# A column sum moved from TensorE to GpSimd, and four PSUM evictions split between ScalarE and GpSimd

## The chip, the cores and the metric

The kernel runs on one core of one Trainium2 chip. The metric is the time of one execution on the device in microseconds (us); the number that stands for a kernel is the median of several runs. A core has five engines with a queue of instructions each, which run in the order in which they were written: TensorE (PE in the profile, with its weight loads as PEld), VectorE (DVE), ScalarE (ACT), GpSimd (POOL) and SyncE (SP, which here only issues DMAs). POOL issues DMAs too. An instruction waits on semaphores for what it needs, and everything behind it on its engine waits with it.

## What is computed

The reference first does a small attention between x (8 batches, 8 heads, 512 positions, 64 wide) and a state of 32 slots, in both directions; its outputs, put together, are 8 x 544 = 4352 rows of 512. On these rows it runs a two-layer network:

```python
h = x @ w_in                 # 512 -> 2048
r = np.maximum(h, 0.0)
g = s * (r * r) + b          # s and b: one number each
return (g @ w_out)           # 2048 -> 512
```

Since b is one number, `g @ w_out` is `s * (r*r) @ w_out + b * colsum(w_out)`, where `colsum` adds the 2048 rows of w_out. The second term is one row of 512 numbers, the same for every output row. The kernel computes it once as `bias_bc`, repeated on all 128 partitions, and adds it where the products leave PSUM.

## The kernel before

The work goes batch by batch (b = 0 to 7). For each batch the attention weights are computed from `xT` (x transposed) and `stT` (`att_scores`, `att_M`), and layer 1 multiplies the weights `a4` with `M` (state times w_in, `L267 ... bank<-a,M` in the profile), which gives h without the attention's output ever being formed. ACT evicts h with a relu (L921), DVE squares it in place (L931): this is `g`, held in f16. Layer 2 multiplies g with w_out, which lies in four tiles `wo[0]` to `wo[3]`, each [128 partitions, 4 blocks, 512 columns] in f16, loaded by four DMAs from POOL's queue (L433).

Batch 0's layer 2 (`layer2_first`, L1134) is a plain product: 16 blocks of w_out times four row blocks `rr`, into two banks of the kind `o` and two of the kind `ps`. The other batches use `layer2` (L1187), a scheme with seven instead of eight block products, which needs sums of blocks of w_out (`weight_sums`, L1040, tile `u`, made by DVE once, line L1051) and of blocks of g (`pair_sums`, L1004, tile `pd`, by DVE, lines L1013, L1021, L1024). What leaves PSUM there is multiplied by s and joined with the bias by DVE (`take`, L1222) or with an earlier part (`give`, L1234), into one of six f32 tiles `osb`, and sent to memory by a DMA (`put`, L1128). The attention's second direction (`att_turn`, `att_reads`) transposes the weights by DMA into `aT` (L835, on SP) and multiplies them with x into a bank `V`; its results are collected in `srd` by a copy on POOL (L880) and pass through the network at the end. Before the transposes of batches 0 and 1 POOL writes two columns of `aT` from `wo[3]` (L828), so that the transposes start after that load.

`bias_sum` (L1086) makes the bias in six operations. PE sums w_out's rows with a weight of ones of 32 columns, sixteen matmuls, four at a time beside each other in the array, so that every column sum stands on 32 partitions four times over in parts (L1101). ACT copies it to f16 (L1102), DVE makes the remainder (L1105), so that two f16 numbers hold the f32 sum. PE adds over the partitions with weights of 1/32 (`thirty2`, L1116), and DVE multiplies with b (L1119).

No order is written by hand. All of this only hands operations to a planner (`Plan`, L27). An operation names the engines that may run it with a cost in us, the keys that it reads and writes, and a priority; a lower number goes first. `order` (L84) walks through time: of the operations that could start earliest it takes the one with the best priority, within a small room, and books its cost:

```python
rank = (t + shy, o.prio, o.n)
if best is None or rank < best[0]:
    best = rank, o, e, t
...
room = t + (self.ROOM if e == "PE" else 0.02)
```

DMAs after 35 us are given 4.4 us to land (`LATE`), and buffers are freed by these planned times. The instructions then stand in each engine's queue in the order of the plan; on the chip they keep it, whatever their true times. A cost in the plan thus moves an instruction's place in the queues, not its time. The priorities around the change: the relus of batch 1 2.51, its squares and products of layer 1 4.01, the sums of `weight_sums` 5.5, `pair_sums` 6, the products of `layer2_first` 9, `put` 20, the L828 copies 30.

Of the kernel before, what the change touches and what calls it, by code (L numbers as in the profile page):

```python
# [26 lines left out]
class Plan:  # L27
# [36 lines left out]
    def op(self, engs, fn, rd=(), wr=(), prio=5, mode=None, dma=0.0, gap=0.0, into=(), lands=None):  # L64

        o = Op(len(self.ops), engs, fn, rd, [*wr, *((u,) for u in into)], prio, mode, dma, gap)
        o.lands = lands
        for key in rd:
            o.before.update(self.wrote[key])
        for key in wr:  # L70
            o.before.update(self.wrote[key])
            o.before.update(self.read[key])
        for key in rd:
            self.read[key].append(o)
        for key in wr:
            self.wrote[key] = [o]
            self.read[key] = []
        o.before.discard(o)
        for u in o.units:
            self.users[u].append(o)  # L80
        self.ops.append(o)
        return o
# [146 lines left out]
def kernel(  # L229
# [10 lines left out]
    nc = tc.nc  # L240
    AF = mybir.ActivationFunctionType
    ALU = mybir.AluOpType

    B, H, S, D = x.shape
    Ns = state.shape[2]
    DM = H * D
    DF = moe_w_in.shape[1]
    P = 128
    NKM = DM // P
    NKF = DF // P  # L250
# [5 lines left out]
    scale = float(1.0 / np.sqrt(D))  # L256
# [6 lines left out]
    def sb(name, shape, dtype=FP16):  # L263
        return pool.tile([P, *shape], dtype, name=name, tag=name)

    def mm(out, lhsT, rhs, start=True, stop=True, tp=None, is_transpose=None):
        return nc.tensor.matmul(  # L267
            out,
            lhsT,
            rhs,  # L270
            start=start,
            stop=stop,
            tile_position=tp,
            is_transpose=is_transpose,
            skip_group_check=True,
        )

    ps = [psum.tile([P, FC], FP32, name=f"bank_{i}", tag=f"bank_{i}") for i in range(6)]
# [18 lines left out]
    plan = Plan()  # L297
# [16 lines left out]
    wo = [sb(f"wo_{q}", [4, DM]) for q in range(4)]  # L314
# [6 lines left out]
    gate = sb("gate", [2])  # L321
    ident16 = sb("ident16", [P])
    bones16 = sb("bones16", [P])
    ones16 = sb("ones16", [Ns])
    thirty2 = sb("thirty2", [P])
    one = sb("one", [1], FP32)
    sb1 = sb("sb1", [2], FP32)
    sb_row = sb("sb_row", [2, P], FP32)
# [1 line left out]
    s_bc, b_bc = sb_bc[:, 0:1], sb_bc[:, 1:2]  # L330
    bias_bc = sb("bias_bc", [DM], FP32)
    wsp = sb("wsp", [2, DM])

    ident_dr = nc.inline_tensor(np.eye(P, dtype=np.float16), name="ident_const")
    bones_dr = nc.inline_tensor(
# [5 lines left out]
    nc.vector.memset(warm, 0.0)  # L341
    nc.vector.memset(ones16, 1.0)
    nc.vector.memset(one, 1.0)
    nc.vector.memset(thirty2, 1.0 / Ns)

    def warm_up():
        mm(ob[1], warm[:, 0:P], warm)
# [7 lines left out]
    def T(u):  # L355
        return plan.tile(u)

    op = plan.op
    K = lambda u, *sub: (u, *sub)
# [105 lines left out]
    for i in range(4):  # L465
# [4 lines left out]
        wr=[K(("bones",))],  # L470
        prio=0,
        lands=8.2,
    )
    for i, src in enumerate((moe_s, moe_b)):
        op(
            {"SP": 0.5},
            lambda e, i=i, src=src: nc.sync.dma_start(sb1[0:1, i : i + 1], src.unsqueeze(0)),
            wr=[K(("sb1", i))],
            prio=0,
# [408 lines left out]
    def g_view(u):  # L888
        return T(u).rearrange("p (f t) -> p f t", f=4)
# [194 lines left out]
        )  # L1084

    def bias_sum():  # L1086
        u = plan.unit(("wsum",), "ps")

        def t(e):
            for i in range(NKF // 4):  # L1090
                for q in range(4):
                    mm(
                        T(u)[32 * q : 32 * q + 32],
                        ones16,
                        wo[i][:, q, :],
                        start=(i == 0),
                        stop=(i == NKF // 4 - 1),
                        tp=(0, 32 * q),
                    )

        op({"PE": 0.87}, t, rd=[K(("wo", q)) for q in range(4)], wr=[K(u)], prio=2, mode="cols")  # L1101
        op({"ACT": 0.52}, lambda e: nc.scalar.copy(wsp[:, 0], T(u)), rd=[K(u)], wr=[K(("hi",))], prio=1)  # L1102
        op(
            {"DVE": 0.66},
            lambda e: nc.vector.tensor_tensor(wsp[:, 1], T(u), wsp[:, 0], ALU.subtract),  # L1105
            rd=[K(u), K(("hi",))],
            wr=[K(("lo",))],
            prio=1,
        )
        v = plan.unit(("bias",), "ps")  # L1110

        def t2(e):
            for i in range(2):
                mm(T(v), thirty2, wsp[:, i], start=(i == 0), stop=(i == 1))

        op({"PE": 0.43}, t2, rd=[K(("hi",)), K(("lo",))], wr=[K(v)], prio=2, mode="full")  # L1116
        op(
            {"DVE": 0.66},
            lambda e: nc.vector.tensor_scalar(bias_bc, T(v), b_bc, None, ALU.mult),  # L1119
            rd=[K(v), K(("b",))],  # L1120
            wr=[K(("bias_bc",))],
            prio=1,
        )

    def put(dst, src, key, prio, last=False):
        op(
            {"SP": 0.6} if last else {"POOL": 0.6},
            lambda e: eng(e).dma_start(dst, src()),  # L1128
            rd=[key],
            prio=prio,  # L1130
            dma=0.75,
        )

    def layer2_first():  # L1134

        us = [plan.unit(("o", 0, i), "o" if i < 2 else "ps") for i in range(4)]

        for q in range(4):
            for f in range(4):
                for rr in range(4):  # L1140

                    def t(e, q=q, rr=rr, f=f):
                        mm(
                            T(us[rr]),
                            g_view(G[0, q])[:, f, P * rr : P * rr + P],
                            wo[q][:, f, :],
                            start=(q == 0 and f == 0),
                            stop=(q == 3 and f == 3),
                        )

                    op(
                        {"PE": 0.2157},
                        t,
                        rd=[K(("wo", q)), K(G[0, q], f // 2)],
                        wr=[K(us[rr])],
                        prio=9 + 0.2 * rr if q == 3 else 9,
                        mode="full",
                    )
        for rr in range(4):
            t = plan.unit(("osb", 0, rr), "osb")  # L1160
            op(
                {"DVE": 0.66},
                lambda e, t=t, rr=rr: nc.vector.scalar_tensor_tensor(  # L1163
                    T(t), T(us[rr]), s_bc, bias_bc, ALU.mult, ALU.add
                ),
                rd=[K(us[rr]), K(("s",)), K(("bias_bc",))],
                wr=[K(t)],
                prio=0,
            )
            put(  # L1170
                out_BSn[0, 0:S].rearrange("(q c) n -> c q n", c=SCH)[2 * (rr % 2) + rr // 2],
                lambda t=t: T(t),
                K(t),
                20,
            )
# [140 lines left out]
    layer1(0)  # L1316
    numbers()
    bias_sum()
    layer2_first()
    layer1(1)  # L1320
    for q in range(4):
# [67 lines left out]
```

## Time and profile before

| | us |
|---|---|
| median of 3 runs (210.03 to 210.66) | 210.12 |
| profiled execution, its own time | 209.61 |
| its span, first to last instruction | 207.8 |
| L267 bank<-wo,ones, 16 matmuls, first start | 31.25 |
| L1102 on ACT | 0.59 |
| L1105 on DVE | 0.68 |
| L1119 on DVE | 0.75 |
| L1163 on DVE, four times, 44.77 to 48.24 | 0.75 each |
| L828 on POOL, four copies, first start | 30.60 |
| L1222, first of `layer2(1)` | 49.11 |

The span is what the trace covers; the 1.8 us beside it are before the first and after the last instruction. Busy times are unions of an engine's instructions. Lines of the timeline give the start, the length, the engine, the line, the operation, what is written and read, and the number of instructions that are merged; consecutive instructions of one engine overlap, so the step from one start to the next is shorter than the length of one. All matmuls have the line L267, a helper's, and are told apart by their tiles. The clock that TensorE was granted is 0.998 of full speed.

### The profile page before, as it was taken

Reading aid. Unit: us, or ns where it says so; the run is one execution under the profiler, and the core shown is the slowest. Engines: PE = TensorE matmul, PEld = TensorE weight load, DVE = VectorE, ACT = ScalarE, POOL = GpSimd, SP = SyncE. Lnnn points to the kernel's source line nnn. Section 1 sums busy time; section 2 is a strip of 40 time slices with the busy share of each in tenths; the row PEclk is TensorE's granted clock in tenths of the full one; section 3 lists DMA queues with packets and bytes.
Section 4 is the critical chain, followed back from the end, with each engine's and each line's share of the span. In section 5 each row is a group of like instructions: output and inputs, shape, how many; then the busy total and the mean of one; then the engine's idle time right before and its main releaser. Section 6 shows DMA issues by size and latency. Waiting matters only on the chain.

```text
span 207.8 us, 4869 instructions
## 1 busy us (share of the span) xinstructions
PE 200.2 (96%) x1968; PEld 132.2 (64%) x1968; DVE 167.3 (80%) x330; ACT 116.7 (56%) x264; POOL 39.4 (19%) x66
## 2 busy tenths in 40 slices
PE   7988999999999999999999999999999999999991
PEld 2434334448864674578477747774777478888881
DVE  1476679999996999999989799988898799684461
ACT  4595699900278689764964596369635953130000
POOL 5930010015113110212301205620105011210000
PEclk9999999999999999999999999999999999999999
DMA  6999999526847843298581841696105101112132
GB/s 187 228 200 206 206 192 150 96 42 175 179 107 155 128 110 78 57 152 195 112 105 58 148 109 52 77 260 79 51 9 162 44 6 50 54 50 101 54 126 76
DMA packets 41930, 24.04 MB, mean 116 GB/s; under 512 B 26292, under 2 KB 40116, under 8 KB 41908
## 3 DMA queue, kind: packets, MB, share of 16 engines
q0 software_dynamic: 15296, 15.40, 38.9%
q1 hardware_dynamic: 25940, 8.17, 19.5%
q8 instruction: 15, 0.25, 0.5%
q10 hardware_dynamic: 672, 0.16, 0.4%
q14 instruction: 7, 0.06, 0.1%
HBM read 17.37 MB, written 8.91 MB: 126 GB/s over the span
## 4 chain that ended last, share of the span: by engine, by line
PE 84%; DMA 8%; DVE 4%; POOL 2%; issue 0%
PE o L267 45%; PE bank L267 39%; DMA wi<-in_moe_w_in_dram 7%; DVE osb L1163 1%; DMA ident<-ident_const 1%; DVE osb L1222 1%; POOL wi L420 1%; DVE pd L1013 1%; POOL xn L407 0%; POOL wo L433 0%; DVE osb L1234 0%; DVE pd L1024 0%; DVE pd L1021 0%; DVE u L1051 0%; POOL gate L457 0%
## 5 line engine op out<-in xcount | busy, mean ns | idle before, releaser
L921 ACT ACTIVATE g<-bank 128x512 f16<-128x512 f32 x128 | 64.3, 653 | 11.6 <-PE bank L267 11.4
L267 PE MATMUL bank<-a,M 128*128 128x512 f16 x256 | 58.2, 379 | 0.3 <-DVE a L785 0.3
L267 PEld LDWEIGHTS <-pd 128*128 128x128 f16 x480 | 46.2, 98 | 10.5 <-issue 3.1
L931 DVE TENSOR_TENSOR g<-g 128x1024 f16<-128x1024 f16 x64 | 43.7, 689 | 8.4 <-ACT g L921 8.4
L267 PEld LDWEIGHTS <-g 128*128 128x128 f16 x424 | 41.0, 98 | 13.6 <-issue 1.3
L267 PE MATMUL o<-u,pd 128*128 128x256 f16 x360 | 43.3, 273 | 0.3 <-DVE osb L1222 0.2
L267 PEld LDWEIGHTS <-M 128*128 128x128 f16 x256 | 24.7, 98 | 29.5 <-issue 1.6
L1128 POOL DMA_DIRECT2D out_dram<-osb x28 | 18.5, 659 | 109.2 <-DVE osb L1234 68.9
L267 PE MATMUL o<-wo,g 128*128 128x256 f16 (+1 forms) x272 | 38.0, 285 | 0.0
L1222 DVE SCALAR_TENSOR_TENSOR osb<-o,sb_bc,bias_bc 128x512 f32<-128x512 f32 (+1 forms) x32 | 22.8, 717 | 8.1 <-PE o L267 7.6
L365 DVE CAST M<-bank 128x512 f16<-128x512 f32 x36 | 23.6, 684 | 4.9 <-PE bank L267 4.9
L726 ACT ACTIVATE E<-bank 128x256 f16<-128x256 f32 x28 | 10.4, 384 | 29.6 <-PE bank L267 29.6
L1234 DVE SCALAR_TENSOR_TENSOR osb<-o,sb_bc,osb 128x512 f32<-128x512 f32 (+1 forms) x24 | 17.2, 715 | 5.7 <-PE o L267 5.6
L365 ACT CAST M<-bank 128x512 f16<-128x512 f32 x28 | 15.3, 596 | 10.2 <-PE bank L267 10.2
L1013 DVE TENSOR_TENSOR pd<-g 128x1024 f16<-128x1024 f16 (+1 forms) x32 | 20.6, 652 | 0.2
L267 PE MATMUL o<-u,g 128*128 128x256 f16 x120 | 15.5, 273 | 0.0
L267 PE MATMUL o<-wo,pd 128*128 128x256 f16 x120 | 15.3, 273 | 0.0
L1024 DVE TENSOR_TENSOR pd<-g,pd 128x512 f16<-128x512 f16 (+1 forms) x32 | 13.0, 409 | 0.1
L1021 DVE TENSOR_TENSOR pd<-g,pd 128x512 f16<-128x512 f16 (+1 forms) x32 | 12.8, 404 | 0.1
L267 PE MATMUL bank<-wi,stT 64*32 64x512 f16 x256 | 10.8, 382 | 1.1 <-DMA wi<-in_moe_w_in_dram 1.1
L976 ACT ACTIVATE g<-bank 128x512 f16<-128x512 f32 x8 | 4.8, 597 | 11.0 <-PE bank L267 11.0
L267 PE MATMUL bank<-wo,g 128*128 128x512 f16 x32 | 9.7, 380 | 0.0
(63 smaller groups left out, 137.4 us busy)
## 6 DMA issues: line engine op xcount, KB each, us to landing
out_dram<-osb POOLq DMA_DIRECT2D x28, 256.0 KB, 3.1
xn<-in_x_dram POOLq DMA_DIRECT2D x7, 512.0 KB, 6.8
wi<-in_moe_w_in_dram POOLq DMA_DIRECT2D x4, 512.0 KB, 11.1
wo<-in_moe_w_out_dram POOLq DMA_DIRECT2D x4, 512.0 KB, 17.8
u<-in_x_dram SPq DMA_DIRECT2D x4, 256.0 KB, 3.8
out_dram<-osb SPq DMA_DIRECT2D x4, 256.0 KB, 2.5
out_dram<-osb SPq DMA_DIRECT2D x4, 128.0 KB, 2.3
xT<-xn SPq DMA_TRANSPOSE x24, 3.2
```

Of the source, the lines that this page charges most:

```text
L267: return nc.tensor.matmul(out, lhsT, rhs, start=start, stop=stop, tile_position=tp, is_transpose=is_transpose, skip_group_check=True,)
L365: (nc.scalar.copy if e == "ACT" else nc.vector.tensor_copy)(dst, src)
L726: lambda e, g=g, m=m: nc.scalar.activation(T(E[b])[:, g, hS * m : hS * m + hS], T(("T", b, m))[:, hS * g : hS * g + hS], AF.Exp, scale=sca ...
L921: lambda e, u=u, j=j, i=i: nc.scalar.activation(g_view(G[b, j])[:, i], T(u), AF.Relu),
L931: nc.vector.tensor_mul(t, t, t)
L976: lambda e, u=u, two=two: nc.scalar.activation(two(), T(u), AF.Relu),
L1013: nc.vector.tensor_tensor(view()[:, :, 0:2], blocks(b, j)[:, :, 1:2, :].to_broadcast((P, 2, 2, n)), blocks(b, j)[:, :, 0:4:3, :], ALU.subt ...
L1021: nc.vector.tensor_tensor(view()[:, :, 2], blocks(b, j)[:, :, 3], view()[:, :, 0], ALU.subtract)
L1024: nc.vector.tensor_tensor(view()[:, :, 3], blocks(b, j)[:, :, 2], view()[:, :, 2], ALU.subtract)
L1128: lambda e: eng(e).dma_start(dst, src()),
L1222: lambda e: nc.vector.scalar_tensor_tensor(t_view(u), o_view(bank), s_bc, bias(h), ALU.mult, ALU.add),
L1234: lambda e: nc.vector.scalar_tensor_tensor(t_view(u), o_view(bank), s_bc, t_view(u), ALU.mult, ALU.add),
```

## The change

`bias_sum` no longer sums on PE. Fifteen additions on POOL run through the sixteen blocks of w_out into an f32 tile `wacc`, which is the memory of `bias_bc`; each reads and writes all of `wacc`. They have the priority 12 and a planned cost of 1.1. Every partition then holds the sum of its own 16 rows, so the two matmuls over the partitions take plain ones as weights and `thirty2` goes. The operations behind have priority 4 where they had 1 or 2.

In `layer2_first` the four products leave PSUM by ACT, multiplied by s alone, into `osb`, and POOL adds `bias_bc` in place (priority 19, planned cost 1.3) before the DMA. `layer2` is not touched.

```diff
-    ones16 = sb("ones16", [Ns])
-    thirty2 = sb("thirty2", [P])
+    ones16 = sb("ones16", [P])
...
+    wacc = bias_bc
...
-    nc.vector.memset(thirty2, 1.0 / Ns)
...
-        op({"PE": 0.87}, t, rd=[K(("wo", q)) for q in range(4)], wr=[K(u)], prio=2, mode="cols")
-        op({"ACT": 0.52}, lambda e: nc.scalar.copy(wsp[:, 0], T(u)), rd=[K(u)], wr=[K(("hi",))], prio=1)
+        blocks_ = [(q, f) for q in range(4) for f in range(4)]
+        for i, (q, f) in enumerate(blocks_):
+            if i == 0:
+                continue
+            one_ = (lambda: wo[0][:, 0]) if i == 1 else (lambda: wacc)
+            op(
+                {"POOL": 1.1},
+                lambda e, q=q, f=f, one_=one_: nc.gpsimd.tensor_tensor(wacc, one_(), wo[q][:, f], ALU.add),
+                rd=[K(("wo", q))],
+                wr=[K(("wacc",))],
+                prio=12,
+            )
+        op({"ACT": 0.52}, lambda e: nc.scalar.copy(wsp[:, 0], wacc), rd=[K(("wacc",))], wr=[K(("hi",))], prio=4)
...
-            lambda e: nc.vector.tensor_tensor(wsp[:, 1], T(u), wsp[:, 0], ALU.subtract),
+            lambda e: nc.vector.tensor_tensor(wsp[:, 1], wacc, wsp[:, 0], ALU.subtract),
...
-                mm(T(v), thirty2, wsp[:, i], start=(i == 0), stop=(i == 1))
+                mm(T(v), ones16, wsp[:, i], start=(i == 0), stop=(i == 1))
...
-                {"DVE": 0.66},
-                lambda e, t=t, rr=rr: nc.vector.scalar_tensor_tensor(
-                    T(t), T(us[rr]), s_bc, bias_bc, ALU.mult, ALU.add
-                ),
-                rd=[K(us[rr]), K(("s",)), K(("bias_bc",))],
+                {"ACT": 0.6},
+                lambda e, t=t, rr=rr: nc.scalar.activation(T(t), T(us[rr]), AF.Copy, scale=s_bc),
+                rd=[K(us[rr]), K(("s",))],
                 wr=[K(t)],
                 prio=0,
+            )
+            op(
+                {"POOL": 1.3},
+                lambda e, t=t: nc.gpsimd.tensor_tensor(T(t), T(t), bias_bc, ALU.add),
+                rd=[K(("bias_bc",))],
+                wr=[K(t)],
+                prio=19,
             )
```

More of the change, by code (lines that the diff above doesn't have):

```diff
@@ L1086, in bias_sum @@
     def bias_sum():
[L1087 to L1099, printed above, removed]
-        op({"PE": 0.87}, t, rd=[K(("wo", q)) for q in range(4)], wr=[K(u)], prio=2, mode="cols")
-        op({"ACT": 0.52}, lambda e: nc.scalar.copy(wsp[:, 0], T(u)), rd=[K(u)], wr=[K(("hi",))], prio=1)
+        blocks_ = [(q, f) for q in range(4) for f in range(4)]
[11 more added lines that the diff above has]
+        op({"ACT": 0.52}, lambda e: nc.scalar.copy(wsp[:, 0], wacc), rd=[K(("wacc",))], wr=[K(("hi",))], prio=4)
         op(
             {"DVE": 0.66},
-            lambda e: nc.vector.tensor_tensor(wsp[:, 1], T(u), wsp[:, 0], ALU.subtract),
-            rd=[K(u), K(("hi",))],
+            lambda e: nc.vector.tensor_tensor(wsp[:, 1], wacc, wsp[:, 0], ALU.subtract),
+            rd=[K(("wacc",)), K(("hi",))],
             wr=[K(("lo",))],
-            prio=1,
+            prio=4,
         )
@@ L1113, in t2 @@
             for i in range(2):
-                mm(T(v), thirty2, wsp[:, i], start=(i == 0), stop=(i == 1))
-        op({"PE": 0.43}, t2, rd=[K(("hi",)), K(("lo",))], wr=[K(v)], prio=2, mode="full")
+                mm(T(v), ones16, wsp[:, i], start=(i == 0), stop=(i == 1))
+        op({"PE": 0.43}, t2, rd=[K(("hi",)), K(("lo",))], wr=[K(v)], prio=4, mode="full")
         op(
@@ L1120, in bias_sum @@
             rd=[K(v), K(("b",))],
-            wr=[K(("bias_bc",))],
-            prio=1,
+            wr=[K(("bias_bc",)), K(("wacc",))],
+            prio=4,
         )
```

## The prediction

> **What bounds the kernel now.** I read the page's busy shares first, then the chain of waits between 40 and 54 us, then the timelines of TensorE (PE), VectorE (DVE) and GpSimd (POOL) in the stretch that the change touches.
>
> The busy shares and the first shares of the chain:
>
> ```profile
> PE 200.2 (96%) x1968; PEld 132.2 (64%) x1968; DVE 167.3 (80%) x330; ACT 116.7 (56%) x264; POOL 39.4 (19%) x66
> ...
> PE 84%; DMA 8%; DVE 4%; POOL 2%; issue 0%
> ```
>
> PE is the bound. The windows show it busy 182.94 of the 183.32 us from 20.38 to 203.70, so a PE instruction that goes is worth its full step, and a wait put into PE's queue costs its full length. The 4% of DVE lie in one place. In the chain's answer for 40 to 54 us (start, length, what):
>
> ```profile
> 44.77 0.75 DVE osb L1163
> 45.52 0.33 DVE u L1051
> 45.86 1.40 DVE osb L1163 x2
> 47.25 0.33 DVE pd L1021
> 47.58 0.66 DVE osb L1163
> ...
> 51.13 0.67 DVE osb L1234
> 51.80 0.04 issue
> 51.84 2.13 PE o L267 x18
> ```
>
> DVE runs without a pause from 44.77, and PE waits at 51.84 for its L1234 (0.15 us). DVE work done before 51.84 therefore has no slack here, although PE itself is hardly idle.
>
> **The PE part.** The timeline of PE around the removed sum:
>
> ```profile
> 29.64 1.67 PE L267 MATMUL bank<-a,M 128*128 128x512 f16 x7
> 31.25 1.05 PE L267 MATMUL bank<-wo,ones 128*32 128x512 f16 x16
> 32.23 1.04 PE L267 MATMUL bank<-a,M 128*128 128x512 f16 x4
> ```
>
> The seven matmuls step by 0.22 us, so the last starts at 30.94 and the next could start at 31.16 instead of 32.23: **1.07 us** less, mode changes included. The later two bias matmuls (34.61, 0.59 us with `thirty2`) stay, with `ones16` as weights. The matmuls behind need `a` (L794, 29.89 to 30.57) and are ready. The memset of `thirty2` (165 ns at the start) goes beside loads and counts nothing.
>
> **The GpSimd additions: their length.** Fifteen additions of 128x512 replace the sixteen matmuls. POOL has no addition in this trace. The low end is DVE's step for a f32 tile of that size, 0.67 us (45.86 to 47.25 holds two). The high end is POOL's own copies: five of 128 columns start between 127.8 and 130.1, 0.58 us apart; four of 2 columns between 30.6 and 31.1, 0.17 apart; the slope, 3.3 ns a column, makes 1.85 us of 512. These copies write with gaps and read one input, an addition writes densely and reads two. I take the middle, 1.3. [...]
>
> When they run: the `wo` loads take 11.5 to 21.0 us to landing. The last lands at 30.5 (issue 9.54 plus 21.0, and POOL's L828 starts at 30.60); the one before, issued at 8.38, at about 28 (the median of 17.8 and its place between put it there). Additions on earlier quarters run from about 17 us and are done by then. The last eight can start at 28: 28 + 8 x 1.3 = 38.4 undisturbed.
>
> **What they do to DVE** decides the case. The one place where POOL computes over more than 2 columns beside DVE shows this (POOL first, then DVE):
>
> ```profile
> 127.77 3.30 POOL L880 COPY srd<-srdT 128x128 f16<-128x128 f16 x5
> ```
> ```profile
> 127.42 0.51 DVE L1021 TENSOR_TENSOR pd<-g,pd 128x512 f16<-128x512 f16 x1
> 127.86 0.88 DVE L931 TENSOR_TENSOR g<-g 128x1024 f16<-128x1024 f16 x1
> ...
> 128.91 0.75 DVE L1222 SCALAR_TENSOR_TENSOR osb<-o,sb_bc,bias_bc 128x512 f32<-128x512 f32 x1
> 129.58 0.68 DVE L365 CAST M<-bank 128x512 f16<-128x512 f32 x1
> 130.17 0.55 DVE L1024 TENSOR_TENSOR pd<-g,pd 128x512 f16<-128x512 f16 x1
> ```
>
> L1021 and L1024 otherwise take 0.42, L931 0.68. The operations with two SBUF inputs are stretched by 0.09, 0.20 and 0.13; those that read PSUM keep their 0.75 and 0.68. A fourth at 170.78 (0.51 instead of 0.42) meets the copy at 171.1. That is about 0.1 us for each copy of 128 columns and one input. An addition reads eight times as many columns, so some 0.75 us of DVE if it lies wholly beside such operations. The ends are 0.1 (a fixed price per instruction) and the whole 1.3; nothing in an added POOL read makes DVE faster, so a gain is excluded. I take 0.75, which scales the row. [...]
>
> From 28 to 41 us DVE is busy 11.9 us (4.17, 4.77 and 5.00 in the windows of 5 us from 28, 33 and 38); less the casts (1.29), `wsp` (0.68) and bias (0.75), about 9.2 of 13 us are two-SBUF operations (L931, L1051, L794), a share of 0.71. Eight additions: 8 x 0.75 x 0.71 = 4.3 us. DVE's idle time there is about 1 us, mostly ahead of 31; I count half as usable: **DVE is 3.8 us late** at 41 us. POOL is held too, by about as much: 28 + 8 x (1.3 + 0.5) = 42.4.
>
> **How this reaches PE.** The queues are written in the order of the planner, which knows no contention and counts 1.1 us per addition. ACT's copy to `wsp` has a lower claim than the relus; ACT's run of relus ends at 41.17, now 40.1. So in the plan: copy 40.1 (0.59), DVE's subtraction (0.68), with two handovers of 0.2, and the bias matmuls at 41.8. Behind them in PE's queue stand the rest of the first batch's layer 2 and all that follows. In truth the subtraction stands behind DVE's late work, 3.8 us late (POOL's chain alone would make it some 2.3 late), and PE waits about **3.8 us** at the bias matmuls. Copy and subtraction now read SBUF instead of PSUM; the nearest rows from SBUF, ACT's 0.71 (L804) and DVE's 0.75 for a f32 tile, differ by 0.1, which I leave out. ACT has nothing else until the four evictions, so its wait costs only them.
>
> **The evictions.** Four DVE operations (0.75, step 0.70) go, 2.8 us, with the idle 0.41 before the first about 3.0 of DVE's queue ahead of 51.84. ACT is idle from 41.17 to 55.75, so four of about 0.6 (`wsp`'s copy: 0.59) are free. Four POOL additions come in 45 to 52, beside DVE's `pd` sums: 4 x 0.75 x 0.7 = 2.1 back. PE would come 1.07 earlier, so of the 3.0 there are 1.9 for it: 0.2 us more late.
>
> **What is moved.** POOL's four L828 copies (30.60) stand behind the additions by their priority, so the four aT transposes on SP come some 12 us later and the V matmuls (40.53) with them; the planner knows that to 37, adds 4.4 us to a landing, and V's result is used at the end: nothing. Output DMAs start after the additions, 2 to 4 us later, x_load of batch 3 (48.10) likewise; its transposes run only at 66: nothing. Six `osb` buffers are held longer, which may hold back one `take` at 55 by 1 to 2 us; other matmuls fill that.
>
> **Sum**: -1.07 + 3.8 + 0.2 = about +3.0 us. The profiled execution (span 207.8, its own time 209.61) would be 212.6; on the runs' median of 210.12 this is **213.1**.
>
> **Rivals.** *The other side: faster.* If a POOL read costs DVE only a fixed 0.1 to 0.2 an instruction, the loss is 8 x 0.15 x 0.71 = 0.9, less 0.5 usable: 0.4 of wait at the bias matmuls, the chain (38.4 and a bit) comes before 40.1, and the relieved DVE removes the 0.15 wait: -1.07 + 0.4 - 0.15 = -0.8, **209.3**; with no wait at all 208.9. It decides from a loss under 0.2 to 0.25 us an addition, and additions under 1.6 us (28 + 8 x 1.6 = 40.8). For it speaks that only about 0.1 was ever seen; against it that it grew with overlap (0.20 beside two copies). Chance 0.27.
> *Exclusion*: each addition takes its 1.3 from DVE: 8 x 1.3 x 0.71 - 0.5 = 6.9, then 4 x 1.3 x 0.7 - 1.9 = 1.7: -1.07 + 8.6 = +7.5, **217.6**. Chance 0.15.
> *It cancels*: the wait eats the 1.07 (loss of 0.3 an addition): 210.1. Chance 0.08.
> *My forecast*, a loss of 0.4 to 0.9 or additions of 1.7 us or more: 211 to 216, chance 0.50.
>
> **The numbers.** The runs tell 0.3% (0.6 us) from no change: faster 0.27, within 0.08, slower 0.65. The range takes in the fast rival and most of exclusion, 208.8 to 217.6; the likeliest case's own is 211 to 216.
>
> **What would show it.** No wo,ones matmuls and a step of 0.22 in their place; POOL additions back to back from 17 us, steps of 1.3 to 1.9 after 28; L931 and L1051 stretched over 0.8 and 0.5 beside them; L1105 after 44 and a PE idle time of 3 to 4 us whose releaser is DVE `wsp`; no PE wait at `pd` beyond 0.5. Wrong if L931 stays at 0.68 to 0.75 beside additions: then PE has no new wait and it is faster. An addition of 2 us or more would make POOL, through ACT's L1102 copy, the releaser.

## The result and the profile after

The changed kernel takes 218.26 us (median of 4 runs, 217.71 to 219.16), the kernel before 210.07 in the same comparison: a ratio of 1.039, 95% interval 1.0367 to 1.0414. The forecast was slower, 213.1, in a range of 208.8 to 217.6. The direction holds, the time lies above the range.

From the page of the changed kernel: the busy times, PE's row and the granted clock in 40 slices, and the chain by engine.

```profile
PE 201.8 (93%) x1952; PEld 132.2 (61%) x1952; DVE 175.1 (81%) x325; ACT 119.6 (55%) x268; POOL 70.1 (32%) x85
PE   7889999909799999999999999999999999999992
PEclk9999999975999999999999999999999999999999
PE 74%; DVE 12%; DMA 7%; POOL 2%; ACT 1%; issue 1%; DVEq 0%
```

PE has 16 instructions less and is busy 1.6 us longer. Its row has one empty slice (43 to 48 us), and the clock falls beside and behind it. DVE's share of the chain has gone from 4 to 12%.

PE's timeline shows where (start, length, what, and in brackets the idle time and what ended it):

```profile
43.09 0.38 PE L267 MATMUL bank<-wsp,ones 128*128 128x512 f16 x1
48.51 0.59 PE L267 MATMUL bank<-wsp,ones 128*128 128x512 f16 x1 [5.04 <-DVE wsp L1102]
48.89 1.49 PE L267 MATMUL o<-wo,g 128*128 128x512 f16 x3
50.17 3.28 PE L267 MATMUL bank<-wo,g 128*128 128x512 f16 x8
...
57.24 0.82 PE L267 MATMUL o<-u,pd 128*128 128x256 f16 x6
59.47 0.84 PE L267 MATMUL bank<-ident,st 128*128 128x128 f16 x12 [1.41 <-DVE st L514]
```

The same places in the kernel before:

```profile
34.61 0.59 PE L267 MATMUL bank<-wsp,thirty 128*128 128x512 f16 x2
45.44 1.89 PE L267 MATMUL bank<-wo,g 128*128 128x512 f16 x8
```

The first bias matmul runs, the second waits 5.04 us for DVE's subtraction (L1102, L1105 before). The eight matmuls into `bank` at 50.17 take 3.28 us; before, the same eight took 1.89. Their step is 0.43 instead of 0.22. The windows give the granted clock of this stretch as 0.50 (half speed):

```profile
core 0: us, PE busy (x) PEld busy (x) DVE busy (x) ACT busy (x) POOL busy (x), PEclk, DMA share, GB/s
46.20:52.90 6.70, 4.39 (x11) 1.61 (x11) 6.70 (x16) 1.38 (x2) 2.36 (x1) 0.50 0.00 0
```

The sum, by starts: 5.42 us from the first bias matmul to the second instead of 0.22, 5.2 lost; 4.56 us for the eleven steps from 48.51 to 53.07 instead of 2.4, 2.2 lost to the clock; 1.57 at 59.47 (six steps of 0.11 behind 57.24 end at 57.90). Against that the removed matmuls: the last matmul of batch 0's layer 1 and the first of batch 1's stand 0.38 us apart (31.05 and 31.43) instead of 1.29 (30.94 and 32.23), 0.91 gained. Together +8.1; the spans differ by 8.1 (215.9 and 207.8).

Why DVE is late stands in POOL's and in its own timeline:

```profile
22.84 16.57 POOL L1094 TENSOR_TENSOR bias_bc<-bias_bc,wo 128x512 f32<-128x512 f32 x12 [1.40 <-DMA wo<-in_moe_w_out_dram]
```
```profile
30.00 1.37 DVE L793 TENSOR_TENSOR a<-E,a 128x1024 f16<-128x1024 f16 x1
31.29 1.37 DVE L1050 TENSOR_TENSOR u<-wo 128x512 f16<-128x512 f16 x1
32.59 1.64 DVE L930 TENSOR_TENSOR g<-g 128x1024 f16<-128x1024 f16 x1
34.15 1.38 DVE L1050 TENSOR_TENSOR u<-wo,u 128x512 f16<-128x512 f16 x1
...
38.31 1.37 DVE L1050 TENSOR_TENSOR u<-wo,u 128x512 f16<-128x512 f16 x1
39.61 0.68 DVE L930 TENSOR_TENSOR g<-g 128x1024 f16<-128x1024 f16 x1
```

The kernel before:

```profile
32.12 0.42 DVE L1051 TENSOR_TENSOR u<-wo 128x512 f16<-128x512 f16 x1
32.46 0.68 DVE L931 TENSOR_TENSOR g<-g 128x1024 f16<-128x1024 f16 x1
33.06 0.68 DVE L1105 TENSOR_TENSOR wsp<-bank,wsp 128x512 f16<-128x512 f32 x1
```

POOL's additions run from 17.16 to 39.40. A sum of w_out blocks (L1050) steps by 1.30 instead of 0.33, a square (L930) by 1.56 instead of 0.60: each pays about 0.96, whatever its own length. The addition steps by 1.23 when nobody disturbs it, by 1.3 to 1.56 here. So the two engines take turns, one DVE operation and one addition, and DVE pays 0.96 of an addition's 1.23 each time. At 39.61, when the additions are over, the square is back at 0.68. Seven operations pay, `a` 0.69 and six of 0.96: 6.4 us.

### The profile page after: what moved, and what is told of

Same layout as the page of the kernel before. It is cut to its first block, busy times and chain, and to the rows that moved or that the text cites. A ratio compares the mean times of both kernels' runs of the same rounds, so it can differ in the third digit from the quotient of the medians.

```text
span 215.9 us, 4866 instructions
## 1 busy us (share of the span) xinstructions
PE 201.8 (93%) x1952; PEld 132.2 (61%) x1952; DVE 175.1 (81%) x325; ACT 119.6 (55%) x268; POOL 70.1 (32%) x85
## 4 chain that ended last, share of the span: by engine, by line
PE 74%; DVE 12%; DMA 7%; POOL 2%; ACT 1%; issue 1%; DVEq 0%
PE o L267 42%; PE bank L267 32%; DMA wi<-in_moe_w_in_dram 6%; DVE g L930 5%; DVE u L1050 3%; DMA ident<-ident_const 1%; DVE osb L1224 1%; POOL wi L419 1%; DVE pd L1020 1%; DVE a L793 1%; DVE M L364 1%; ACT g L920 1%; ACT bank L769 0%; POOL xn L406 0%; DVE pd L1012 0%
## 5 line engine op out<-in xcount | busy, mean ns | idle before, releaser
L920 ACT ACTIVATE g<-bank 128x512 f16<-128x512 f32 x128 | 64.5, 654 | 14.0 <-PE bank L267 13.8
L267 PE MATMUL bank<-a,M 128*128 128x512 f16 x256 | 58.9, 379 | 0.5 <-DVE a L784 0.5
L930 DVE TENSOR_TENSOR g<-g 128x1024 f16<-128x1024 f16 x64 | 48.1, 755 | 9.7 <-ACT g L920 9.7
L267 PE MATMUL o<-wo,g 128*128 128x256 f16 (+1 forms) x272 | 39.2, 288 | 0.0
L1224 DVE SCALAR_TENSOR_TENSOR osb<-o,sb_bc,bias_bc 128x512 f32<-128x512 f32 (+1 forms) x32 | 22.7, 714 | 9.9 <-PE o L267 9.0
L1094 POOL TENSOR_TENSOR bias_bc<-bias_bc,wo 128x512 f32<-128x512 f32 x14 | 18.7, 1334 | 2.4 <-DMA wo<-in_moe_w_out_dram 1.4
L267 PE MATMUL o<-wo,pd 128*128 128x256 f16 x120 | 14.6, 273 | 0.0
L1020 DVE TENSOR_TENSOR pd<-g,pd 128x512 f16<-128x512 f16 (+1 forms) x32 | 13.7, 435 | 0.0
L1023 DVE TENSOR_TENSOR pd<-g,pd 128x512 f16<-128x512 f16 (+1 forms) x32 | 13.5, 426 | 0.1
L1167 POOL TENSOR_TENSOR osb<-osb,bias_bc 128x512 f32<-128x512 f32 x4 | 8.3, 2110 | 8.9 <-DVE bias_bc L1116 8.9
```

The lines of the kernel that those rows point to most:

```text
L267: return nc.tensor.matmul(out, lhsT, rhs, start=start, stop=stop, tile_position=tp, is_transpose=is_transpose, skip_group_check=True,)
L920: lambda e, u=u, j=j, i=i: nc.scalar.activation(g_view(G[b, j])[:, i], T(u), AF.Relu),
L930: nc.vector.tensor_mul(t, t, t)
L1020: nc.vector.tensor_tensor(view()[:, :, 2], blocks(b, j)[:, :, 3], view()[:, :, 0], ALU.subtract)
L1023: nc.vector.tensor_tensor(view()[:, :, 3], blocks(b, j)[:, :, 2], view()[:, :, 2], ALU.subtract)
L1094: lambda e, q=q, f=f, one_=one_: nc.gpsimd.tensor_tensor(wacc, one_(), wo[q][:, f], ALU.add),
```

## The experiments

Three theories stand against each other: **E**, exclusion, as just read; **C**, the chain of additions is simply too slow for those who wait for the sum; **P**, **O** and **S**, the loss comes from the new order of the queues, from the evictions and output DMAs, or from the later transposes. In all kernels of this section the 48 DMA transposes on SP are plain DMAs of the same tiles, so the transposition is left out. Ratios are to the kernel before, on the same chip.

**The base.**

```diff
-   nc.sync.dma_start_transpose(T(aT[b])[:, g], T(E[b])[:, g])
+   nc.sync.dma_start(T(aT[b])[:, g].rearrange("p c q -> p (c q)"), T(E[b])[:, g])
...
```

> The kernel before, with its 48 DMA transposes (xT of batches 2 to 7, aT, srdT) as plain DMAs of the same tiles on the same queue: the transposition is left out, so the attention's data are not those of the reference. It is the base for the other kernels of this kind. No transpose stands on the chain that ended last, so all theories expect 209.3 to 211.

Measured: 210.24 us, ratio 0.9975 (0.9944 to 1.0006). The plain DMAs make no difference that can be measured.

> The changed kernel with the same 48 DMAs plain. Theory E (exclusion: while a GpSimd addition runs, a DVE operation with two SBUF inputs does not get on, so DVE loses about 1 us to each of some seven additions, PE waits for DVE's subtraction at the bias matmuls, and its clock is halved for a while behind that wait) and theory C (chain: the additions are too slow, the bias comes late): 216.5 to 219.5, with a PE wait of 4.5 to 5.5 us at the bias matmuls. If the later transposes make the loss (theory S): under 213.

Measured: 218.68 us, ratio 1.0361 (1.0289 to 1.0433), the wait at the bias matmuls 5.04 us as in the changed kernel. The loss is there without a transposition. That the later start of these DMAs does not make it either shows below: in `plain_write_only` POOL's copies ahead of them (L827) stand behind the memsets, which end at 43.6 (in the changed kernel they start at 39.35), and PE waits for none of these DMAs. S falls.

**The parts.** The sum alone, with L1163's DVE evictions put back:

```diff
-                {"ACT": 0.6},
-                lambda e, t=t, rr=rr: nc.scalar.activation(T(t), T(us[rr]), AF.Copy, scale=s_bc),
...
+                {"DVE": 0.66},
+                lambda e, t=t, rr=rr: nc.vector.scalar_tensor_tensor(
+                    T(t), T(us[rr]), s_bc, bias_bc, ALU.mult, ALU.add
+                ),
...
```

> The changed kernel, DMAs plain, with the four evictions as before (one DVE operation each, no GpSimd addition on osb); the column sum stays on GpSimd. Theories E and C: the wait of some 5 us at the bias matmuls and the half clock behind it stay: 216 to 219. Theory O (the evictions and what they move, the output DMAs, make most of the loss): 211 to 213.

Measured: 219.69 us, ratio 1.0421 (1.0357 to 1.0485), again a wait of 5.0 us for `wsp`. The sum alone makes the loss. The evictions alone (the same lines the other way round, in the kernel before):

> The kernel before, DMAs plain, with the four evictions of the change (ScalarE, then a GpSimd addition); the column sum stays on PE. Theory E: DVE gains 3.0 us at 44 to 48 and loses 0.7 to 1.0 to each of two to four additions beside its pair sums: 209.5 to 212, and a first addition on osb that waits while DVE's operations follow each other closely. Theory C says nothing of it: 209.9 to 210.3. Theory O: 214 or more.

Measured: 211.71 us, ratio 1.0035 (0.9991 to 1.0079). With more rounds:

> The evictions of the change alone once more, DMAs plain, with more rounds. Theory E: one DVE operation stretched by about 1 us, PE waits of 0.4 us: 210.0 to 211.2, no gain, since PE had not waited for these four DVE operations by more than 0.15 us.

Measured: 211.34 us, ratio 1.0047 (1.0018 to 1.0076), a small loss, slightly over the expected times. As the maker of most of the loss, O falls. In the trace of `plain_evict_only` one DVE operation that touches only SBUF meets an addition and is stretched, a copy with a single input that otherwise takes 0.35 (53.31 in the kernel before), and PE waits 0.4 us for it:

```profile
51.53 1.42 DVE L515 COPY st<-st 128x768 f16<-128x768 f16 x1
```

**Additions that nobody waits for.** C and E part where the additions are made but not used:

```diff
+    spare = sb("spare", [DM])
...
+        for i, (q, f) in enumerate([(q, f) for q in range(4) for f in range(4)][1:]):
+            one_ = (lambda: wo[0][:, 0]) if i == 0 else (lambda: spare)
+            op(
+                {"POOL": 1.1},
+                lambda e, q=q, f=f, one_=one_: nc.gpsimd.tensor_tensor(spare, one_(), wo[q][:, f], ALU.add),
+                rd=[K(("wo", q))],
+                wr=[K(("spare",))],
+                prio=12,
+            )
```

> The kernel before, DMAs plain, with the fifteen GpSimd additions put in beside it, into an f16 tile that nobody reads; the sum on PE, the bias and the evictions are those of before. Theory E: the operations with two SBUF inputs (L931's squares, L1051's sums) step by 1.3 to 1.6 us instead of 0.33 to 0.60 from 30 to 40 us, DVE is about 6 us late, PE waits for it at the bias matmuls or at the pair sums: 214 to 219. Theory C (nobody waits for the sum, so it costs nothing): 209.5 to 211.5.

Measured: 217.9 us, ratio 1.0365 (1.0335 to 1.0395). The sum is still made by PE, and PE waits for DVE's subtraction all the same, now at 39.95:

```profile
PE bank L267 <- DVE wsp L1106: 4.1, 1, 4.1
```

The columns are the time waited, how often and the longest. Nobody reads `spare`, so C cannot explain it, E does.

**Writing without reading.** The other way round, the waits on POOL stay, and POOL does not read:

```diff
-   lambda e, q=q, f=f, one_=one_: nc.gpsimd.tensor_tensor(wacc, one_(), wo[q][:, f], ALU.add),
+   lambda e: [nc.gpsimd.memset(wacc, 1.0) for _ in range(3)],
```

> The changed kernel, DMAs plain, in which each of the fifteen additions is three memsets of the same tile, so that GpSimd only writes: the column sum is left out and the bias is made of a constant. The order of all queues and every wait on GpSimd are those of the change. Theory E: the squares stay at 0.68 to 0.75 and L1050 at 0.42, no wait over 1 us at the bias matmuls, clock full; what the evictions cost remains: 209 to 212. Theory C (if three memsets last about as long as an addition) and theory P (the new order of the queues makes the loss): 216 to 220.

Measured: 214.85 us, ratio 1.0226 (1.018 to 1.0271): neither theory's time. The 45 memsets step by 0.58 and end at 43.6, later than the additions did, in the same order of the queues. Yet DVE is undisturbed beside them and PE's waits at the bias matmuls are 0.3 and 0.35 us: for the sum C and P fall. What is left sits in the other part. DVE's timeline, first beside the memsets, then beside the four additions on `osb` (47.05 to 52.80):

```profile
32.20 0.69 DVE L930 TENSOR_TENSOR g<-g 128x1024 f16<-128x1024 f16 x1 [0.27 <-ACT g L920]
32.80 0.42 DVE L1050 TENSOR_TENSOR u<-wo,u 128x512 f16<-128x512 f16 x1
...
47.15 1.76 DVE L1012 TENSOR_TENSOR pd<-g 128x1024 f16<-128x1024 f16 x1
48.83 1.49 DVE L1023 TENSOR_TENSOR pd<-g,pd 128x512 f16<-128x512 f16 x1
50.25 1.49 DVE L1020 TENSOR_TENSOR pd<-g,pd 128x512 f16<-128x512 f16 x1
51.66 1.74 DVE L1012 TENSOR_TENSOR pd<-g 128x1024 f16<-128x1024 f16 x1
```

Here all four additions take turns with the pair sums, 1.07 us each, 4.3 in all, and PE waits 3.7 us for a `take` (L1224). The expectation had taken the price of the evictions from the changed kernel, where only two pair sums were hit, and was wrong in that.

**No reads at all.** Two memsets per addition, and the additions on `osb` left out:

> The changed kernel, DMAs plain, with no GpSimd operation that reads: each addition of the sum is two memsets (the column sum is left out, a constant takes its place), and the four additions on osb are left out (the first batch goes without its bias). What is left of the change is the sixteen matmuls less and the evictions on ScalarE. Theory E: no DVE operation stretched, no PE wait over 0.5 us between 22 and 200 us, the step of 1.07 us gone from PE: 208.7 to 209.6 where the kernel before has 210.1. If the order of the queues or the late bias costs by itself (theory P): 210.5 to 213.

Measured: 208.19 us, ratio 0.9899 (0.9866 to 0.9931), faster than expected. All that PE waits for in this trace lies in the first 22 us:

```profile
PE bank L267 <- DMA wi<-in_moe_w_in_dram: 1.5, 2, 1.0
PE o L267 <- DVE warm L341: 1.2, 1, 1.2
PE bank L267 <- DVE xT L364: 0.3, 1, 0.3
```

Without POOL's reads the rest of the change gains 1.0%; with them it loses 3.6% (`plain_after`). From the first matmul of batch 1's layer 1 to the last matmul it is 0.8 us shorter than in the kernel before: of that 0.32 and 0.35 are the two PE waits of the kernel before that are gone, at 51.84 and at 84.38. This kernel leaves out the column sum and the first batch's bias.

**Size and place.** Half as many columns, then only the seven early additions (both against `plain_adds_unread`):

```diff
-   nc.gpsimd.tensor_tensor(spare, one_(), wo[q][:, f], ALU.add)
+   nc.gpsimd.tensor_tensor(spare[:, 0:256], one_(), wo[q][:, f, 0:256], ALU.add)
...
```

> The kernel before, DMAs plain, with fifteen unread additions of 256 columns instead of 512. Theory E as the traces put it (each blocked DVE operation waits for one whole addition, whatever its own length): the stretch of L1051 and L931 falls from about 0.96 to 0.45 to 0.6 each, the PE wait at the bias matmuls from 4.1 to under 1 us: 210.5 to 213.5. If the price is fixed per addition: 216 to 218.

Measured: 212.92 us, ratio 1.0129 (1.0093 to 1.0165), PE's wait 1.3 us where under 1 was expected.

```profile
31.70 1.16 DVE L932 TENSOR_TENSOR g<-g 128x1024 f16<-128x1024 f16 x1
32.78 0.89 DVE L1052 TENSOR_TENSOR u<-wo,u 128x512 f16<-128x512 f16 x1
33.59 0.89 DVE L1052 TENSOR_TENSOR u<-wo 128x512 f16<-128x512 f16 x1
```

A square takes 1.16, a sum 0.89: 0.47 over their own 0.68 and 0.42, both the same, and half of 0.96. The price grows with the addition's columns, with hardly a fixed part.

```diff
-        for i, (q, f) in enumerate([(q, f) for q in range(4) for f in range(4)][1:]):
+        for i, (q, f) in enumerate([(q, f) for q in range(2) for f in range(4)][1:]):
```

> The kernel before, DMAs plain, with seven additions only, on the first two quarters of w_out, into a tile that nobody reads; they run from 17 to 28 us, where DVE is idle for a third of the time. Theory E: two to four squares stretched by 0.4 to 1.0 each, some 2.5 us in all, of which DVE's idle time takes up most: 210 to 211.3. If an addition costs the kernel its share wherever it stands: 7/15 of 7.7, so 213.5 to 214.

Measured: 210.09 us, ratio 1.000 (0.9979 to 1.0021). Squares are stretched here too (two of them last 2.70 together at 23.64, where each took 0.69), but DVE had time to spare: in the kernel before it is busy 7.39 of the 11 us from 17 to 28. Seven additions cost nothing that can be measured.

**The clock.** 23 matmuls of a zero tile fill PE's wait:

```diff
         def t2(e):
+            for _ in range(23):
+                mm(T(v), warm[:, 0:P], warm)
             for i in range(2):
```

> The changed kernel, DMAs plain, with 23 matmuls of a zero tile ahead of the bias matmuls in PE's queue, 5.0 us at full clock, into the bank that the bias matmuls then start afresh. They lie in the time in which PE waits for DVE. If the half clock behind the wait comes from PE standing still (theory H): no half clock at 48 to 53, ten matmuls at 0.22 instead of 0.43 a step, 1.5 to 2.3 us less than the changed kernel with plain DMAs (218.7): 216.3 to 217.3. If the clock falls for another reason: 218.5 to 219.5.

Measured: 216.99 us, ratio 1.0335 (1.0279 to 1.0392); against `plain_after` the intervals overlap, so the times do not decide it. The timelines do: the eight matmuls of the stretch, first with the filling, then in `plain_after`.

```profile
49.95 1.89 PE L267 MATMUL bank<-wo,g 128*128 128x512 f16 x8
```
```profile
51.59 2.51 PE L267 MATMUL bank<-wo,g 128*128 128x512 f16 x8
```

With the filling there is no half clock in the middle of the run (a mean of 0.998 against 0.991). So here it is the standing still that brings the half clock. In `plain_after` it lasts 3.41 us, half as long as in the changed kernel's 6.83, so there was less to win than the expectation said.

**Telling the planner.** The costs that the trace showed, so that only the order changes:

```diff
-                {"DVE": 0.34},
+                {"DVE": 1.3 if q == 0 else 0.34},
...
-                {"POOL": 1.1},
+                {"POOL": 1.4},
...
```

> The changed kernel, DMAs plain, with the planner told what the trace showed: 1.3 for the product into a4 of batch 1 and the four weight sums of the first quarter, 1.56 for two squares of batch 1, 1.4 for an addition. Only the order of the queues changes; DVE's subtraction for the bias stands some fifteen DVE operations earlier. Theory E, with DVE's lost time as the cause wherever PE waits: the wait at the bias matmuls falls under 1.5 us, and PE waits for weight sums and pair sums behind it instead: 213 to 217. If the place of the subtraction were the cause (theory Q): 209.5 to 212.

Measured: 221.15 us, ratio 1.0495 (1.0447 to 1.0542), slower still and outside both ranges. PE's timeline:

```profile
45.06 0.38 PE L267 MATMUL bank<-wsp,ones 128*128 128x512 f16 x1 [0.76 <-DVE wsp L1102]
...
56.71 3.59 PE L267 MATMUL o<-u,pd 128*128 128x256 f16 x16 [5.38 <-DMA srdT<-sr]
```

The wait at the bias matmuls has shrunk to 0.76, and PE stands 5.38 us at the first product that needs a pair sum. The releaser is misnamed: the DMA writes `srdT`, which these matmuls do not read, while their weight loads wait for DVE `pd`. So the place of the subtraction was not the cause (Q falls): the lost DVE time came out where PE next needed DVE. The total is above what E foresaw, since in this order the additions on `osb` also took turns with DVE (two sums of w_out blocks, L1050, last 1.49 and 1.48 from 49.31 on, where one alone takes 0.41), which the expectation had left out.

## Why the prediction was wrong

**Direction and place: right.** PE lost its time at the bias matmuls, waiting for DVE's subtraction, as forecast (a wait of 3 to 4 us, a start after 44; measured 5.04 and 47.78), and the cause was contention of POOL's reads with two-SBUF operations (1.37 for 0.42 beside reads, 0.42 beside memsets). The additions' length was about right too: 1.3 taken, a step of 1.23 alone and 1.3 to 1.56 in turns measured; an addition of 2 us or more, the sign that POOL itself is too slow, did not occur in the column sum. The PE term was 1.07 foretold, 0.91 measured, the rest lost to `a`, which was 0.69 late.

**How much came from where.** The forecast added 3.0 us, the runs 8.1. Of the 5.1 between them 1.4 lie in the wait (3.8 foretold, 5.2 lost), 2.2 in the clock, 1.4 in the evictions and 0.2 in the PE term.

**The step that failed** is "8 x 0.75 x 0.71 = 4.3": the price of an addition to DVE, taken as a stretch in proportion to the overlap and thinned by the share of two-SBUF operations. The runs show turns in its place. Of the seven two-SBUF operations that came while an addition ran, six paid 0.96, a short one as much as a long one; being held, DVE spent nearly all its time in such operations (all seven from 30.00 to 39.61), so the share drops out. Seven operations paid 6.4 us, not 4.3; about half of the difference is the price (0.96 for 0.75), half the share. Scaling the row by columns was not the fault, since half the columns paid half (0.47). The row itself, stretches of 0.09 to 0.20 beside copies, could not tell a share from turns. The second rival, exclusion, had the mechanism and a chance of 0.15, and the range ended at its own sum, 217.6. That this sum came near 218.26 is partly luck: its wait, 6.9 where 5.2 was lost, made up for most of the clock, which it left out too.

**A term was missing**: the clock, the largest of the four. The prediction priced PE's wait at its length. Behind it eleven steps ran at half clock, 2.2 us.

**The evictions** were priced at 0.2; 1.57 was lost at 59.47. Two pair sums were stretched by 0.69 and 1.07, 1.8 of the 2.1 foretold; but the 3.0 us by which DVE was to be relieved did not help, since DVE, at 55.78, had itself stood idle 1.90 us for the late PE, and behind that PE was in step with DVE and had no slack. That DVE's relief is worth little the runs confirm: alone, the evictions cost 0.5%.

**What hides**: moved transposes and DMAs cost nothing, as forecast (`plain_write_only`, `plain_no_reads`). The faster rival needed a loss under 0.25 us an addition; its 208.9 for no wait at all was reached only without reads (208.19).

**Which operations pay**, as far as the runs show it: beside memsets none did (0.69 and 0.42 in `plain_write_only`), and the casts from PSUM did not (0.67 to 0.69 in the whole changed kernel, three of them beside additions, from 26.03). The copy L515, with one SBUF input, did pay (1.42 for 0.35 in `plain_evict_only`), and no run shows why.

## What to carry to other kernels

GpSimd's additions from SBUF were not beside the work here while DVE was busy with two-SBUF operations: price such an addition at nearly its whole length per DVE operation that it meets (0.96 of 1.23 us here), and put it where DVE has idle time (seven additions between 17 and 28 us were free) or make it shorter. Look for the first instruction in PE's queue that needs the delayed engine, since an order that was written ahead stands still there, and changing that place only moved the wait (from 5.04 us at the bias matmuls to 5.38 at the first product that needs a pair sum). Price a long wait of PE (3.7 us or more here) with the matmuls behind it at half clock.

## What the runs showed of the hardware

- The half clock lasted 6.83 us in the changed kernel (a granted clock of 0.50 from 46.15, inside the wait of 5.04) and 3.41, half of that, in `plain_after` (0.50 from 49.42, near the end of the same wait). It came with PE waits of 3.7 (`plain_write_only`, mean clock 0.989), 4.1 (`plain_adds_unread`, 0.989), 5.0 (the changed kernel, 0.984) and 5.4 us (`plain_informed`, 0.984); with waits of 1.3 (`plain_half`, 1.000), 1.4 (the changed kernel from 58 to 63, 1.00) and 2.2 (`plain_warm`, 0.998 as in the kernel before) there was none in the middle of the run.
- Who goes first was not fixed. In the changed kernel the first addition on `osb` took from 50.54 to 55.0, while DVE's sums ran at full speed until DVE itself went idle (53.9):

```profile
50.54 5.69 POOL L1167 TENSOR_TENSOR osb<-osb,bias_bc 128x512 f32<-128x512 f32 x2 [8.93 <-DVE bias_bc L1116]
```

  The two additions last 5.69 where two alone take 2.5. In `plain_evict_only` it was much the same (8.43 us for all four, 8.32 in the changed kernel). In `plain_write_only` the first addition, which also came during a pair sum (47.05), was let in at once: none of the four lasted more than 1.71. Which of the two happens, and so whether the evictions hit two pair sums or four, no run settled.
